# New scheduling priorities for a fused sketch-attention and tanh-shrink kernel

## The chip, the cores and the metric

The kernel runs on one core of a Trainium2 chip. The metric is the time of one execution in microseconds on the device. The time before is the median of three runs.

## The reference

Attention by a polynomial sketch comes first, then a two-layer network on its output. All inputs and the output are float32.

```python
def phi(x):                                   # x: [4, 4, 1088, 32] (batch, head, token, 32)
    a = einsum('rd,bhsd->bhsr', S1, x)        # S1, S2: [8, 32]
    b = einsum('rd,bhsd->bhsr', S2, x)
    return einsum('bhsi,bhsj->bhsij', a, b).reshape(..., 64)
q_p, k_p = phi(q), phi(k)
kv  = einsum('bhsf,bhsd->bhfd', k_p, v)
z   = sum(k_p, axis=2)
num = einsum('bhsf,bhfd->bhsd', q_p, kv)
den = einsum('bhsf,bhf->bhs', q_p, z)[..., None] + 1e-6
x   = (num / den) as [4352, 128]              # tokens x (heads * 32)
h   = x @ w_in                                # w_in: [128, 2048]
out = (h - tanh(h)) @ w_out                   # w_out: [2048, 128]
```

## The kernel before

**What is computed where.** The network is split by linearity: `out = x @ (w_in @ w_out) - tanh(h) @ w_out`. The product of the two weights is formed once, in two bf16 parts (`whi`, `wlo`). So each block of tokens needs matmuls for h (TensorE, line 898), tanh (ScalarE, line 902, with a scale of -1), matmuls of the tanh with `w_out` (line 912), and two linear matmuls with `whi` and `wlo` (line 889).

**Stages.** The 4352 tokens are handled in 11 *layers* of 8 to 14 times 32 tokens (256 to 448 columns). A layer g has 16 blocks jb of the hidden width. The program names its steps by tags, which the text below uses too:

- `h{g}_{jb}`: the matmul of layer g, block jb, into one of three PSUM banks that are used in turn (4, 5, 6). It has to wait until the tanh of three blocks before has left the bank.
- `t{g}_{jb}`: its tanh, into one of 40 slots in SBUF.
- `y{g}_{jb}`: the matmul of the tanh with `w_out`, added up in PSUM bank 7. The linear matmuls are added into the same bank. `o{g}` on VectorE (line 920) turns the sum to the output's layout; four transfers on the queue of SyncE store it.
- The last two layers, 9 and 10, are made in rows of 128 tokens (line 933): `y{g}_{jb}_{y}` and `l{g}_{y}whi`, `l{g}_{y}wlo` for row y, the linear part. Their tokens lie in the last group of the attention, so all of them read what `x8` writes.

The attention feeds this in 9 *groups* of tokens: `qT{g}` transposes q on VectorE (line 695), `p{g}` projects (TensorE, line 717), `qq`, `au`, `dn`, `ds`, `dt`, `rd`, `an`, `qp` and `qpT` (lines 746 to 799, VectorE and GpSimd) make the products and the scaling, `w{g}` (TensorE, line 733) makes the numerators, and `x{g}` (VectorE, line 812) copies them as bf16 into `xT`, which the h and l matmuls read. For `x8`, the last group, the copy has a pattern of its own: it puts the tokens in the order that the rows of the last layers need.

For each of the four batches b there is work on the keys: `kT{b}0`, `kT{b}1` (transposes, VectorE, line 601), `kp{b}` (TensorE, line 608), `kab{b}` (VectorE, line 619), `kps` (line 625), `wk{b}{t}` (products, VectorE and GpSimd, line 634), `gram{b}`, `gm{b}`, `fold{b}`, `u{b}` (lines 645 to 660), `sums{b}` (TensorE, line 673), `kvz{b}`, `turn{b}`, `ndw{b}` (ScalarE and TensorE, lines 681 to 687).

**What sets the order.** Each step is recorded with an engine, a cost in ns, a priority and what it reads and writes. A list scheduler (`listed`) in the kernel's own code then goes through a model of the time: on each engine it takes, of the steps that are ready by the model, the one with the lowest priority value. The order that comes out is fixed in the program; every engine then takes its instructions in that order, with semaphore waits where a step needs one of another engine. Priorities come from the place of a step (for example 16 g + jb for `h`, and 12 more for `y`), and at the end a table adds a shift to some of them:

```python
for tag, by in SHIFT.items():
    P.tags[tag].prio += by
```

The costs that the model uses are formulas; that of a copy on VectorE is

```python
def dve(n):
    return 100 + n / 0.96
```

and `x{g}` is entered at `dve(32 * nb) - 35`, with nb = 20 for `x8`. Some sequences are laid down by hand with `P.line([...])`; these are the same in both kernels.

Of the kernel before, what the change touches and what calls it, by code (L numbers as in the profile page):

```python
# [45 lines left out]
class Program:  # L46
# [210 lines left out]
    def emit(self):  # L257
# [64 lines left out]

SHIFT = {
# [21 lines left out]
}  # L345
TURNED = (0, 1, 3)

# [717 lines left out]
```

## Time and profile before

| | before |
|---|---|
| runs | 102.39, 102.39, 102.28 us; median 102.39 |
| profiled execution | 102.28 us, of which 100.5 are the span of its instructions |
| busy: TensorE, ScalarE, VectorE, GpSimd | 96.5, 78.0, 71.5, 33.2 us |
| matmuls | 1231 |
| tanh instructions (line 902) | 168, 71.9 us |
| granted TensorE clock | 0.996 |

In the profile PE is TensorE's matmuls and PEld its weight loads, DVE is VectorE, ACT ScalarE, POOL GpSimd and SP SyncE. A timeline row has its start and its length in microseconds, the engine, the line in the kernel, the operation with its tiles, and the number of instructions that were merged into the row; in brackets stands the idle time of the engine before it and what ended that. A matmul's length runs to the end of its result, and the next one starts well before that: the pace of PE is read from the starts. A row of the table by stages has start:end, length, and for each engine the busy time with the number of instructions.

### The profile page before, as it was taken

How to read it: one execution, taken by the hardware profiler on the slowest of the kernel's cores; microseconds unless marked ns; L12 is line 12 of the kernel's file. 1: busy time of each engine (PE TensorE's matmuls, PEld its weight loads, DVE VectorE, ACT ScalarE, POOL GpSimd, SP SyncE). 2: the span in 40 equal slices, each digit the busy share in tenths (PEclk: the TensorE clock that was granted, in tenths of full speed). 3: DMA queues.
4: the chain of work that ended last, by engine and by line, in shares of the span. 5: the costliest groups of instructions: out<-in, count | busy, mean ns of one | idle time of the engine just before them, and what ended most of it. 6: DMA issues, size and time to landing. Idle time of an engine off the chain costs nothing.

```text
span 100.5 us, 3032 instructions
## 1 busy us (share of the span) xinstructions
PE 96.5 (96%) x1231; PEld 52.0 (52%) x1231; DVE 71.5 (71%) x181; ACT 78.0 (78%) x182; POOL 33.2 (33%) x60
## 2 busy tenths in 40 slices
PE   6999999999999999999999999999999999999980
PEld 5446467544666444545544444455444444468970
DVE  3689977999869999978999999899577226002140
ACT  0005679998957849793899998898999999999960
POOL 5577388042842400596040029403018000000000
PEclk9999999999999999999999999999999999999998
DMA  2899978920389451310899032002201403100512
GB/s 77 284 281 236 382 237 290 325 66 4 71 285 231 121 91 26 52 33 0 258 273 231 5 49 42 7 0 39 45 14 22 69 0 60 25 0 12 98 42 75
DMA packets 22510, 11.21 MB, mean 112 GB/s; under 512 B 16096, under 2 KB 21216, under 8 KB 22496
## 3 DMA queue, kind: packets, MB, share of 16 engines
q1 hardware_dynamic: 18976, 7.44, 30.5%
q10 hardware_dynamic: 3520, 3.57, 11.5%
q8 instruction: 9, 0.15, 0.6%
q14 instruction: 5, 0.04, 0.1%
HBM read 8.78 MB, written 2.23 MB: 110 GB/s over the span
## 4 chain that ended last, share of the span: by engine, by line
PE 87%; DMA 5%; DVE 4%; ACT 2%; issue 1%; POOL 0%; POOLq 0%; DVEq 0%
PE ps L898 31%; PE ps L912 24%; PE ps L733 5%; PE ps L933 5%; PE ps L673 5%; PE ps L717 4%; PE ps L608 3%; PE ps L889 3%; DMA kraw<-in_k_dram 3%; ACT tt L902 2%; DMA out_dram<-osl 2%; DVE wk L634 1%; PE ps L547 1%; PE ps L849 1%; PE ps L645 1%; PE ps L684 1%
## 5 line engine op out<-in xcount | busy, mean ns | idle before, releaser
L902 ACT ACTIVATE tt<-ps 128x448 bf16<-128x448 f32 (+3 forms) x168 | 71.9, 544 | 6.5 <-PE ps L898 6.0
L898 PE MATMUL ps<-xT,w_in 128*128 128x448 bf16 (+2 forms) x176 | 50.7, 333 | 0.2
L912 PE MATMUL ps<-tt,w_out 128*128 128x448 bf16 (+2 forms) x144 | 39.3, 338 | 0.0
L898 PEld LDWEIGHTS ps<-xT,w_in 128*128 128x128 bf16 x176 | 16.2, 98 | 20.4 <-ACT tt L902 11.5
L634 POOL TENSOR_TENSOR wk<-kab 128x256 f32<-128x256 f32 (+1 forms) x18 | 12.2, 675 | 19.1 <-DVE kab L619 17.5
L792 POOL TENSOR_TENSOR qp<-an,qq 128x512 f32<-128x512 f32 (+5 forms) x12 | 12.4, 1033 | 18.4 <-DVE an L780 17.5
L912 PEld LDWEIGHTS ps<-tt,w_out 128*128 128x128 bf16 x144 | 14.1, 98 | 7.7 <-issue 0.5
L920 DVE STREAM_TRANSPOSE osb<-ps 128x448 f32<-128x448 f32 (+1 forms) x8 | 5.0, 627 | 11.4 <-PE ps L912 11.4
L799 DVE STREAM_TRANSPOSE qpT<-qp 128x448 f32<-128x448 f32 (+5 forms) x18 | 11.4, 658 | 0.3 <-POOL qp L792 0.2
L933 PE MATMUL ps<-w_out,tt 128*128 128x128 bf16 x80 | 8.1, 219 | 0.0
L681 ACT ACT_TABLE_LOAD x1 | 1.3, 1283 | 8.3 <-issue 8.3
L1035 POOL MEMSET mark<- 128x1 f32 x1 | 0.1, 99 | 22.3 <-DMA out_dram<-osl 22.3
L746 DVE STREAM_TRANSPOSE qq<-ps 128x448 f32<-128x448 f32 (+5 forms) x9 | 6.0, 671 | 1.7 <-PE ps L717 1.5
L547 PE MATMUL ps<-const-bfloat16-1.0 128*128 128x256 bf16 (+1 forms) x25 | 6.5, 394 | 0.8 <-PEq L1050 0.8
L812 DVE CAST xT<-ps 128x448 bf16<-128x448 f32 (+4 forms) x8 | 6.2, 773 | 1.5 <-PE ps L733 1.4
L933 PEld LDWEIGHTS ps<-w_out,tt 128*128 128x128 bf16 x80 | 6.4, 98 | 0.6
L601 DVE STREAM_TRANSPOSE kT<-kraw 128x576 f32<-128x576 f32 (+1 forms) x8 | 5.7, 730 | 1.0 <-DMA kraw<-in_k_dram 0.9
L695 DVE STREAM_TRANSPOSE qT<-qraw 128x448 f32<-128x448 f32 (+5 forms) x9 | 5.9, 654 | 0.2 <-DMA qraw<-in_q_dram 0.2
L733 PE MATMUL ps<-qpT,ndw 64*32 64x288 f32 (+5 forms) x144 | 5.7, 373 | 0.0
L717 PE MATMUL ps<-qT,wq 64*32 64x288 f32 (+5 forms) x144 | 5.7, 373 | 0.0
L634 DVE TENSOR_TENSOR wk<-kab,ps 128x512 f32<-128x512 f32 x8 | 5.4, 673 | 0.0
L673 PEld LDWEIGHTS ps<-wk,vx 128*32 128x32 f32 x288 | 4.3, 110 | 1.8 <-issue 1.6
(86 smaller groups left out, 89.0 us busy)
## 6 DMA issues: line engine op xcount, KB each, us to landing
kraw<-in_k_dram SPq DMA_DIRECT2D x3, 544.0 KB, 4.1
qraw<-in_q_dram SPq DMA_DIRECT2D x3, 544.0 KB, 6.0
vx<-in_v_dram SPq DMA_DIRECT2D x10, 144.0 KB, 4.2
out_dram<-osb SPq DMA_DIRECT2D x20, 56.0 KB, 1.9
w_in_f<-in_moe_w_in_dram ACTq DMA_DIRECT2D x2, 512.0 KB, 8.1
w_out_f<-in_moe_w_out_dram ACTq DMA_DIRECT2D x2, 512.0 KB, 8.9
vx<-in_v_dram SPq DMA_DIRECT2D x4, 112.0 KB, 5.6
out_dram<-osb SPq DMA_DIRECT2D x8, 48.0 KB, 1.9
```

The costliest lines, as they stand in the source:

```text
L547: P.op("tensor", 213 if x < 12 else 290, lambda e, n=1 if x < 16 else 2: e.matmul(ps[:, 3, 0:256 * n], ones[:, 0:128], ones[:, None, :].to ...
L634: P.op(eng, 60 + 64 * n if eng == "vector" else pool(64 * n), lambda e: e.tensor_tensor(out=wk[:, t0:t1, :, :].rearrange("p t h (i j) -> p ...
L673: ins = e.matmul(ps[32 * h:32 * h + 32, sbk, 0:64], vx[i][:, h, t, :], wk[:, t, h, :], start=(t == 0), stop=(t == 8), tile_position=(0, 32 ...
L717: ins = e.matmul(o, wq[64 * r:64 * r + 64, b, y, :, :].rearrange("p h x -> p (h x)"), src, start=True, stop=True, tile_position=(64 * r, 3 ...
L733: ins = e.matmul(ps[32 * h:32 * h + 32, 2 + u, 0:32 * nh], ndw[i][64 * u:64 * u + 64, 32 * h:32 * h + 32], src[64 * u:64 * u + 64, h // 2, ...
L792: P.op("vector" if dv else "gpsimd", 95 + 33.2 * m if dv else pool(32 * m), lambda e, lo=lo, dv=dv: e.tensor_tensor(out=qp[u][:, lo:lo + m ...
L799: P.op("vector", dve(32 * m), lambda e, lo=lo: e.transpose(out=qpT[u][:, 32 * lo:32 * (lo + m)], in_=qp[u][:, lo:lo + m, :].rearrange("p n ...
L812: P.op("scalar" if early else "vector", (act if early else dve)(32 * nb) - 35, lambda e: (e.copy if early else e.tensor_copy)(xT[:, x0:x0 ...
L898: P.op("tensor", two * pe(n), lambda e, jb=jb, bk=bk: [e.matmul(bk[:, n * x:n * x + n], w_in[:, 128 * (jb + x):128 * (jb + x) + 128], xT[: ...
L902: P.op("scalar", act(n * two), lambda e, ts=ts, bk=bk: e.activation(out=tt[:, ts:ts + two, 0:n], in_=bk[:, 0:n * two].rearrange("p (x n) - ...
L912: P.op("tensor", pe(n), lambda e, jb=jb, ts=ts: e.matmul(acc[:, 0:n], w_out[:, jb, :], tt[:, ts, 0:n], start=(jb == 0 and g < 2), stop=(jb ...
L933: P.op("tensor", 56, lambda e: e.matmul(ps[:, banks[y], 0:128], lhs, rhs, start=first, stop=last), r=r, w=[bank[banks[y]]], prio=prio, tag ...
```

## The change

Only the table `SHIFT` differs. Of its 148 values 22 change, and 47 entries are added; no step, cost, dependency or hand-written sequence does. The six lines that the table grows by move every later line number by 6. Cut to what the text below speaks of:

```diff
-    "h2_7": 11.5, "h2_10": 11.7, "h2_14": 24.1, "y2_9": 22.0, "y2_12": 26.7, "ds4": -2.0, "kT21": 7.6, "kab2": -3.3,
-    "h3_8": -6.6, "y3_4": 44.0, "y3_9": 63.1, "p5": 35.0, "an5_1": -16.5, "sums20": 321.1, "turn2": 92.7, "h4_9":
+    "h2_7": 42.8, "h2_10": 11.7, "h2_14": 24.1, "y2_9": 48.2, "y2_12": 26.7, "ds4": 8.7, "kT21": 7.6, "kab2": -3.3,
+    "h3_8": -6.6, "y3_4": 44.0, "y3_9": 63.1, "p5": 35.0, "an5_1": -16.5, "sums20": 321.1, "turn2": 54.2, "h4_9":
...
-    "p8": 5.8, "y8_0": 12.1, "y8_7": 22.9, "h9_7": 5.4, "h9_11": -10.6, "h9_13": 26.6, "y9_2_0": 29.9, "y9_7_0":
+    "p8": 59.8, "y8_0": 12.1, "y8_7": 22.9, "h9_7": 5.4, "h9_11": 5.9, "h9_13": 26.6, "y9_2_0": 29.9, "y9_7_0":
...
-    "y10_14_0": 4.3,
+    "y10_14_0": 4.3, "wk10": 46.4, "wt1": -14.5, "ndw1": 10.1, "h2_3": 18.1, "dn4": 11.0, "wk26": -13.6, "gram2":
+    -10.2, "t4_9": -3.9, "y4_3": 43.2, "h5_7": 31.7, "h5_14": 34.2, "y5_7": 30.6, "y6_8": 47.0, "y8_1": 30.7,
+    "y8_8": 30.1, "y9_2_2": -31.1, "y9_7_2": 59.8, "l10_0whi": -8.1, "l10_0wlo": 23.7, "l10_1whi": -5.4, "l10_1wlo":
+    9.3, "y10_7_1": 18.0, "y10_13_1": 54.3, "h2_15": 3.0, "y2_5": 32.5, "w3": -34.1, "kT20": 16.3, "kp2": 267.2,
...
```

What this does to the order: the instructions of each engine stay the same ones. On TensorE the order is the same up to `sums10`, about 30.7 us. On VectorE it changes in two places: `x3`, `qT5`, `kT21` and `o2` go ahead of steps that they followed, and `dn6` goes ahead of `x5`. GpSimd takes `wk26` in the place of `wk24`. ScalarE takes some tanh in another order, and `ndw1` and `ndw2` at other places. The transfers on SyncE's queue keep their order. On TensorE many `h`, `y` and `l` matmuls change places with neighbours, `turn2` and `turn3` go ahead of `p6` and `p8`, and behind `w8` the rows of the last layers are placed anew.

23 rows, old and new, of the table SHIFT are left out of this document.

## The prediction

> **What bounds the kernel now.** I began with the page: its span, the shares of the engines, the chain that ended last and the groups.
>
> ```profile
> span 100.5 us, 3032 instructions
> PE 96.5 (96%) x1231; PEld 52.0 (52%) x1231; DVE 71.5 (71%) x181; ACT 78.0 (78%) x182; POOL 33.2 (33%) x60
> ...
> PE 87%; DMA 5%; DVE 4%; ACT 2%; issue 1%; POOL 0%; POOLq 0%; DVEq 0%
> ...
> L902 ACT ACTIVATE tt<-ps 128x448 bf16<-128x448 f32 (+3 forms) x168 | 71.9, 544 | 6.5 <-PE ps L898 6.0
> ```
>
> The chain runs through PE for 87% of the span. But that is an average, so I looked at the stages next (start and end, length, then busy time and count of each engine).
>
> ```profile
> 30.00:40.00 10.00, 10.00 (x147) 5.05 (x136) 9.69 (x24) 7.60 (x19) 1.91 (x2) 1.00 0.53 123
> 80.00:90.00 10.00, 10.00 (x79) 5.00 (x77) 2.18 (x2) 9.86 (x25) 0.00 (x0) 1.00 0.13 21
> 90.00:95.00 5.00, 5.00 (x64) 4.18 (x62) 0.94 (x2) 5.00 (x17) 0.00 (x0) 1.00 0.30 49
> ```
>
> From 30 to 40 us PE has no gap and ACT is idle for 2.4 us of 10: PE alone sets the pace. From 80 us on both are full. There is no slack left for a PE wait to hide in, on either engine. The timeline of ACT shows how far back that goes (start, length).
>
> ```profile
> 71.49 0.27 ACT L687 COPY ndw<-ps 128x128 f32<-128x128 f32 x1
> 71.68 20.72 ACT L902 ACTIVATE tt<-ps 128x448 bf16<-128x448 f32 x50
> ...
> 83.49 3.54 ACT L902 ACTIVATE tt<-ps 128x448 bf16<-128x448 f32 x8
> ```
>
> From 71.68 us tanh follows tanh. The last row is a shorter window of the same stretch: 3.54 us for 8 tanh is 0.55 for the first and about 0.43 for each that follows.
>
> **What the change can win.** No instruction is added or removed; only the order differs. On PE it is the same until 30.7 us. PE's work is thus the same sum, and the change can only take away waits that PE has now, or add some. The waits of now show as matmuls of 448 columns that start more than 0.19 us after the one before:
>
> ```profile
> 43.32 0.35 PE L898 MATMUL ps<-xT,w_in 128*128 128x448 bf16 x1
> ...
> 44.15 0.36 PE L898 MATMUL ps<-xT,w_in 128*128 128x448 bf16 x1
> ```
>
> Three more such matmuls lie between. The four steps take 0.83 us where 4 x 0.19 = 0.76 would do: 0.07 us lost. Going through the starts of all matmuls up to 83 us I find this cluster and three that are no larger, so at most 0.3 us is to be won there:
>
> ```profile
> 75.62 0.55 PE L898 MATMUL ps<-xT,w_in 128*128 128x384 bf16 x2
> 76.10 0.61 PE L733 MATMUL ps<-qpT,ndw 64*32 64x224 f32 x16
> ```
>
> This one, two matmuls of 384 columns that take 0.48 us ahead of w7, lies where ACT is full. In the changed order the turn of batch 3 (turn3, L684) comes before p8, so its copy on ACT (ndw3, the first row of the ACT timeline above) has its input earlier and holds the following tanh back less. I take 0.06 us as the gain, with bounds 0 and 0.3.
>
> **The moves on VectorE, 36 to 41 us.** Here x3, qT5, kT21 and o2 move up, past dn4, ds4 and dt4.
>
> ```profile
> 36.31 0.76 DVE L812 CAST xT<-ps 128x576 bf16<-128x576 f32 x1
> ...
> 37.77 0.80 DVE L769 COPY ps<-dn 32x32 f32<-32x32 f32 x4
> ...
> 39.24 0.73 DVE L695 STREAM_TRANSPOSE qT<-qraw 128x576 f32<-128x576 f32 x1
> ...
> 39.97 0.57 DVE L920 STREAM_TRANSPOSE osb<-ps 128x384 f32<-128x384 f32 x1
> 40.46 0.74 DVE L619 STREAM_TRANSPOSE kab<-ps 128x576 f32<-128x576 f32 x1
> ...
> 29.34 0.43 SPq L503 DMA_DIRECT2D qraw<-in_q_dram  x1
> ...
> qraw<-in_q_dram SPq DMA_DIRECT2D x1, 544.0 KB, 5.0
> ...
> 39.46 0.71 PE L608 MATMUL ps<-kT,wkm 64*32 64x288 f32 x16
> ```
>
> kab2 is the one that PE waits for next. What precedes it is the same set of instructions, so it starts at about 40.5 us again if nothing waits. Two things could. First, x3 is now issued before dn4, while it still needs w3; w3 is one matmul of layer 2 earlier (0.16 us), and I make the idle time that is left 0 to 0.14 us. Second, qT5 needs batch 2's q: its load was issued at 29.34 and landed 5.0 us later, at 34.3, and qT5 now comes near 36.9. It waits for nothing, and 2.5 us cover it. PE gets one matmul more ahead of kp2, so kab2 has its input at 39.46 + 0.19 + 0.71 = 40.4 us. I take 0 here, bounds 0 and 0.14. The other moves on PE up to 83 us change h and y matmuls of neighbouring blocks about. I added up their starts in the new order, 0.19 us for each of 448 columns, and held them against the ends of the tanh that free their banks: none comes late by more than 0.06 us, and where one does, a wait of now goes. They cost nothing by this sum. The moves on GpSimd swap wk24 with wk26, of equal size, and cost nothing, as sums20 waits for all of them.
>
> **The move that costs: the tail of layer 8.** The old order on PE after w8 (L733) and the new one, by the program's names:
>
> ```
> before: h8_9 . h8_10 . h8_11 y8_0 h8_12 y8_1 h8_13 y8_2 h8_14 y8_3 l9_1whi h8_15 l9_1wlo y8_4 h9_0
> after:  h8_9 . h8_10 . h8_11 y8_0 h8_12 l9_1whi l9_1wlo h8_13 l10_0whi l10_1whi y8_1 h8_14 y8_2 h8_15 y8_3 y8_4 h9_0
> ```
>
> A dot is a linear matmul of layer 8. The four l matmuls moved up read xT of the last two layers, which is written by x8, the cast after w8 on VectorE:
>
> ```profile
> 82.39 0.77 PE L733 MATMUL ps<-qpT,ndw 64*32 64x320 f32 x16
> 83.09 0.36 PE L898 MATMUL ps<-xT,w_in 128*128 128x448 bf16 x1
> ...
> 84.23 0.35 PE L898 MATMUL ps<-xT,w_in 128*128 128x448 bf16 x1
> 84.42 0.35 PE L912 MATMUL ps<-tt,w_out 128*128 128x448 bf16 x1
> 84.61 0.35 PE L898 MATMUL ps<-xT,w_in 128*128 128x448 bf16 x1
> ...
> 85.37 0.22 PE L933 MATMUL ps<-whi,xT 128*128 128x128 bf16 x1
> 85.42 0.35 PE L898 MATMUL ps<-xT,w_in 128*128 128x448 bf16 x1
> ...
> 85.86 0.33 PE L898 MATMUL ps<-xT,w_in 128*128 128x384 bf16 x1
> ```
> ```profile
> 83.27 1.59 DVE L812 CAST xT<-ps 128x640 bf16<-128x640 f32 x1 [0.31 <-PE ps L733]
> ```
>
> x8 ends at 83.27 + 1.59 = 84.86 us. Now l9_1whi starts at 85.37, half a microsecond after it. In the new order its place comes right after h8_12 (84.23), at 84.42: 0.44 us before xT is there. PE takes its instructions in order, so h8_13, which needs nothing from x8, stands behind that wait. How soon PE goes on after VectorE is seen at another such wait, o2: it ended at 39.97 + 0.57 = 40.54, and the weight load that waited for it started at 40.59:
>
> ```profile
> 40.59 0.10 PEld L889 LDWEIGHTS ps<-xT,whi 128*128 128x128 bf16 x1 [0.18 <-DVE osb L920]
> ```
>
> So l9_1whi starts at about 84.92, and PE waits 0.50 us. The planner in the code counts x8 at 100 + 640/0.96 - 35 = 732 ns and would see no wait there; the trace has 1,592 ns.
>
> [...]
>
> **What the wait does to the end.** h8_13 comes after the two l matmuls of layer 9 (0.055 us each, as from 85.37 to 85.42): 84.92 + 0.11 = 85.03, against 84.61 now. Then h8_14 comes at 85.03 + 0.19 + 0.11 + 0.19 = 85.52, h8_15 at 85.90, h9_0 at 86.47, and on in this way. How long a tanh takes from its matmul is read where ACT was idle before it:
>
> ```profile
> 47.24 0.73 PE L898 MATMUL ps<-xT,w_in 128*128 128x448 bf16 x3
> ...
> 47.63 0.98 ACT L902 ACTIVATE tt<-ps 128x448 bf16<-128x448 f32 x2 [0.78 <-PE ps L898]
> ```
>
> The first of the three matmuls started at 47.24 and the first tanh at 47.63: 0.39 us. ACT reaches the tanh of h8_13 at 83.49 + 4 x 0.43 = 85.2 now. In the new order its input allows 85.03 + 0.39 = 85.42: ACT idles for 0.2 us. The tanh of h8_14 can start at 85.91, 0.05 later than ACT could; h9_0 and then h9_4, which stands behind two matmuls of y8, add about 0.05 each. After h9_4 the three banks of h set the pace again. ACT is then 0.35 us late. The other 0.15 us of the wait is absorbed, since PE had been ahead of the banks there. ACT is full from there to the end, so the 0.35 us stay.
>
> The end itself changes too:
>
> ```profile
> 96.44 0.28 PE L898 MATMUL ps<-xT,w_in 128*128 128x256 bf16 x1
> 96.56 1.11 PE L933 MATMUL ps<-w_out,tt 128*128 128x128 bf16 x17
> ...
> 97.54 0.49 DVE L942 COPY osl<-ps 128x128 f32<-128x128 f32 x2 [0.99 <-PE ps L933]
> ```
>
> After the last h (96.44, freed by ACT) PE now has 17 row matmuls; in the new order 19 are left. Two more at 0.055 us put the last copy 0.11 us later.
>
> **The sum.** -0.06 (waits that go) + 0 (VectorE) + 0.35 (x8) + 0.11 (rows) = +0.40 us. The profiled execution took 102.28 us, its span 100.5 and 1.78 around it; it would take 102.68. It is the lowest of the runs, 0.11 below their median, so I forecast 102.39 + 0.40 = 102.8 us.
>
> **The rivals.** (1) The wait for x8 is not there, or ACT doesn't feel it. For it: the same instruction at 576 columns needs far less, and x8 may have been slow in this one execution. Against it: the long cast is the only one with the strided pattern of the last group in the code, so I expect the 1.59 us each time. Then -0.06 + 0.11 = +0.05: 102.4 us.
>
> ```profile
> L812 DVE CAST xT<-ps 128x576 bf16<-128x576 f32 x2 | 1.5, 758 | 0.1
> ```
>
> (2) Faster: the earlier stages win all the 0.3 us and x8 is no obstacle either; then -0.3 + 0.11 = -0.19, and 102.2 us. It decides if x8 ends before 84.37 us, since only then l9_1whi finds it done. (3) Slower by more: x3 holds up VectorE by 0.14 us, fold2 and w4 are late by as much, and on top comes the whole wait of 0.50, if PE was not ahead after all: 0.14 + 0.50 + 0.11 = 0.75, or 103.1 us. For it speaks that qpT40 is ready only 0.18 us before w4 takes it:
>
> ```profile
> 43.85 1.30 DVE L799 STREAM_TRANSPOSE qpT<-qp 128x512 f32<-128x512 f32 x2
> ...
> 45.33 0.64 PE L733 MATMUL ps<-qpT,ndw 64*32 64x256 f32 x16
> ```
>
> Against it: the PE waits that go just ahead of w4 (0.07 us, above) would pay half of the delay.
>
> **How the numbers follow.** Forecast 60%, rival 1 20%, rival 2 10%, rival 3 10%. The range runs from rival 1 with a small credit, 102.35, to rival 3, 103.15; that leaves rival 2 and a little of each end out. A difference of 0.2% (0.2 us) is about what a measurement here can tell from none. Slower by more: most of the forecast (0.54), rival 3 (0.10) and the upper end of rival 1 (0.04): 0.68. Within: the rest of the forecast and most of rival 1, 0.20. Faster: rival 2 and the lower end of rival 1, 0.12.
>
> **What would show it.** In the new profile: right after h8_12 a weight load of whi that waited about 0.45 us for the cast of xT on VectorE; an idle stretch of 0.2 us on ACT near 85.2 us, in the midst of what is now one unbroken row; 19 row matmuls behind the last h. Up to 83 us the two timelines should agree within 0.15 us. The prediction is wrong if l9_1whi starts without a wait, or if the last h comes at 96.4 us in spite of it.

## The result and the profile after

| | before | changed |
|---|---|---|
| runs | 15, median 102.39 us | 15, median 102.80 us |
| ratio of the two | | 1.004, 95% interval 1.0023 to 1.0057 |
| profiled execution | 102.28 us, span 100.5 | 103.18 us, span 101.4 |

The kernel is slower by 0.4%, and a ratio of 1 lies outside the interval. The forecast was 102.8 us. The two profiled executions differ by more than the medians, 0.9 us, so they can't be set side by side as they stand. The page of the changed kernel shows what is new in its chain:

```profile
PE 89%; DVE 5%; ACT 2%; DMA 2%; issue 1%; POOL 0%; POOLq 0%
PE ps L904 30%; PE ps L918 24%; PE ps L739 5%; PE ps L939 5%; PE ps L679 5%; PE ps L553 5%; PE ps L723 4%; PE ps L614 3%; PE ps L895 3%; ACT tt L908 2%; DMA out_dram<-osl 2%; DVE xT L818 2%; DVE wk L640 1%; PE ps L855 1%; PE ps L651 1%; PE ps L841 1%
```

`DVE xT L818 2%` is the cast x8 (every line number is 6 higher now; in the kernels of the experiments the numbers differ again, and the tiles tell which line it is). Its 1.58 us lie on the path that sets the end; in the chain before, no cast of VectorE was listed. PE's timeline shows the place, the weight loads and VectorE's cast with it:

```profile
84.50 0.35 PE L918 MATMUL ps<-tt,w_out 128*128 128x448 bf16 x1
84.69 0.35 PE L904 MATMUL ps<-xT,w_in 128*128 128x448 bf16 x1
85.36 0.23 PE L939 MATMUL ps<-whi,xT 128*128 128x128 bf16 x1 [0.32 <-DVE xT L818]
85.42 0.22 PE L939 MATMUL ps<-wlo,xT 128*128 128x128 bf16 x1
85.48 0.35 PE L904 MATMUL ps<-xT,w_in 128*128 128x448 bf16 x1
```
```profile
85.35 0.10 PEld L939 LDWEIGHTS ps<-whi,xT 128*128 128x128 bf16 x1 [0.72 <-DVE xT L818]
```
```profile
83.72 1.58 DVE L818 CAST xT<-ps 128x640 bf16<-128x640 f32 x1 [0.31 <-PE ps L739]
```

h8_12 starts at 84.69 and l9_1whi at 85.36: 0.67 us, of which 0.19 are h8_12 itself. PE waited 0.48 us (the bracket has 0.32, as the result of h8_12 still runs out in that time; that of the weight load has 0.72, as the load before it, for h8_12, had ended earlier). The cast ended at 83.72 + 1.58 = 85.30, and the weight load came 0.05 us after it.

**Where to count from.** The order is the same up to sums10, yet sums10 starts at 30.07 us in this profile and at 29.53 in the one before. That 0.5 us is not the change's. I count from the start of sums10 to the end of the last row matmul in each profile:

```profile
29.53 1.21 PE L673 MATMUL ps<-wk,vx 128*32 128x64 f32 x72
```
```profile
30.07 1.21 PE L679 MATMUL ps<-wk,vx 128*32 128x64 f32 x72
...
97.23 0.28 PE L904 MATMUL ps<-xT,w_in 128*128 128x256 bf16 x1
97.35 1.23 PE L939 MATMUL ps<-w_out,tt 128*128 128x128 bf16 x19
```

Before: 96.56 + 1.11 - 29.53 = 68.14 us. Changed: 97.35 + 1.23 - 30.07 = 68.51 us. The change costs 0.37 us in this count, near the 0.41 of the medians. With the 0.54 us up to sums10 it makes up the 0.9 us between the two profiled executions. The last row also shows the 19 row matmuls behind the last h, in the place of 17.

### The profile page after: what moved, and what is told of

Its sections match the earlier page's. It is cut to its first block, busy times and chain, and to the rows that moved or that the text cites. A ratio compares the mean times of both kernels' runs of the same rounds, so it can differ in the third digit from the quotient of the medians.

```text
span 101.4 us, 3031 instructions
## 1 busy us (share of the span) xinstructions
PE 97.0 (96%) x1231; PEld 52.2 (51%) x1231; DVE 71.5 (71%) x181; ACT 78.3 (77%) x182; POOL 33.2 (33%) x60
## 4 chain that ended last, share of the span: by engine, by line
PE 89%; DVE 5%; ACT 2%; DMA 2%; issue 1%; POOL 0%; POOLq 0%
PE ps L904 30%; PE ps L918 24%; PE ps L739 5%; PE ps L939 5%; PE ps L679 5%; PE ps L553 5%; PE ps L723 4%; PE ps L614 3%; PE ps L895 3%; ACT tt L908 2%; DMA out_dram<-osl 2%; DVE xT L818 2%; DVE wk L640 1%; PE ps L855 1%; PE ps L651 1%; PE ps L841 1%
## 5 line engine op out<-in xcount | busy, mean ns | idle before, releaser
L818 DVE CAST xT<-ps 128x448 bf16<-128x448 f32 (+4 forms) x8 | 6.2, 771 | 1.7 <-PE ps L739 1.7
L939 PE MATMUL ps<-w_out,tt 128*128 128x128 bf16 x80 | 7.3, 219 | 0.0
```

Source lines behind the costliest of these rows:

```text
L818: P.op("scalar" if early else "vector", (act if early else dve)(32 * nb) - 35, lambda e: (e.copy if early else e.tensor_copy)(xT[:, x0:x0 ...
L939: P.op("tensor", 56, lambda e: e.matmul(ps[:, banks[y], 0:128], lhs, rhs, start=first, stop=last), r=r, w=[bank[banks[y]]], prio=prio, tag ...
```

## The experiments

Theory A is the one of the prediction: the l matmuls moved up wait for x8. B puts the loss into the moves between 31 and 83 us or into the early loads. C says that the new tail costs as a whole, whatever those four matmuls do. Three columns tell them apart: the ratio of times, the count from sums10 in one profile, and x8's length there.

| kernel | ratio to before (95%) | from sums10 to the end, against before (us) | x8 (us) |
|---|---|---|---|
| changed | 1.004 (1.0023 to 1.0057) | 68.51, +0.37 | 1.58 |
| changed, old tail | 0.9997 (0.9972 to 1.0022) | 68.07, -0.07 | 1.59 |
| before, new tail | 1.0026 (1.0005 to 1.0046) | 68.59, +0.45 | 1.58 |
| changed, four l back | 0.9991 (0.9965 to 1.0017) | 68.17, +0.03 | 1.58 |
| changed, x8 dense | 0.9999 (0.9974 to 1.0024) | 68.16, +0.02 | 0.82 |
| before, four l early | 1.0051 (1.0024 to 1.0077) | 68.70, +0.56 | 1.58 |
| before, x8 dense | 0.9995 (0.9972 to 1.0017) | 68.13, -0.01 | 0.82 |
| changed, planner knows x8 | 0.9999 (0.9978 to 1.0020) | 68.10, -0.04 | 1.59 |
| changed, x8 twice | 1.0170 (1.0145 to 1.0194) | 69.86, +1.72 | 1.59 and 1.61 |
| before, four l early, h8_13 ahead | a single run, no interval | 68.70, +0.56 | 1.58 |

**The two halves of the change.** In the kernels that have another tail, TensorE's order behind h8_12 is exchanged after the planner has run (`TAIL` lists the names in the order wanted):

```diff
         order = self.schedule()
+        pe = order["tensor"]
+        at = pe.index(self.tags["h8_12"]) + 1
+        moved = [self.tags[x] for x in TAIL]
+        assert set(moved) == set(pe[at:])
+        order["tensor"] = pe[:at] + moved
         self.sync(order)
```

The changed kernel with the old tail:

> The changed kernel with the old order of TensorE behind h8_12 (all other orders as changed). Theory A (the l matmuls stand waiting for x8, and two more rows are left at the end): the whole loss lies behind h8_12, 0.35 + 0.11 us, and the stages before it are 0.06 to 0.09 us quicker than in the kernel before. So 0.05 to 0.1 us below the kernel before, ratio about 0.999, against 1.004 for the change. Theory B (the loss comes from the moves between 31 and 83 us, or from the early loads): it stays at about +0.4 us, ratio 1.004.

The kernel before with the new tail:

> The kernel before with the new order of TensorE behind h8_12, and nothing else of the change. Theory A: the wait of about 0.5 us of l9_1whi for x8 appears here too, and 0.35 + 0.11 = 0.46 us are lost: ratio 1.0045. Theory B: no difference from the kernel before, ratio 1.000.

The loss went with the tail, both ways: -0.07 us without it, +0.45 us with nothing but it. The two profiles:

```profile
29.65 1.21 PE L697 MATMUL ps<-wk,vx 128*32 128x64 f32 x72
...
96.61 1.11 PE L957 MATMUL ps<-w_out,tt 128*128 128x128 bf16 x17
```
```profile
29.54 1.21 PE L691 MATMUL ps<-wk,vx 128*32 128x64 f32 x72
...
96.79 0.28 PE L916 MATMUL ps<-xT,w_in 128*128 128x256 bf16 x1
96.91 1.22 PE L951 MATMUL ps<-w_out,tt 128*128 128x128 bf16 x19
```

B falls. The times agree, less sharply: the ratio of the kernel before with the new tail, 1.0026, is 0.27 us, with 0.05 to 0.47 as its interval. The 0.07 us of gain in the earlier stages shows only in this count; the interval of the times can't tell it from none.

**Only the four l matmuls put back.** l9_1whi and l9_1wlo stand around h8_15 again, l10_0whi and l10_1whi ahead of l10_1wlo; the rest of the new tail stays.

> The changed kernel with only four matmuls put back: l9_1whi and l9_1wlo around h8_15 as before, l10_0whi and l10_1whi ahead of l10_1wlo. Theory A: the wait for x8 goes and with it 0.35 us; the 0.11 us for two more rows at the end stay, and so does the gain of 0.06 to 0.09 in the earlier stages: +0.02 to +0.05 us, ratio about 1.000. Theory C (the rest of the new tail, the y8 matmuls put off and the rows, costs as much by itself): +0.3 to +0.4 us, ratio 1.003 to 1.004.

```profile
84.09 0.65 PE L922 MATMUL ps<-xT,w_in 128*128 128x448 bf16 x2
84.58 0.35 PE L936 MATMUL ps<-tt,w_out 128*128 128x448 bf16 x1
84.81 0.36 PE L922 MATMUL ps<-xT,w_in 128*128 128x448 bf16 x1
85.01 0.35 PE L936 MATMUL ps<-tt,w_out 128*128 128x448 bf16 x1
85.20 0.22 PE L957 MATMUL ps<-whi,xT 128*128 128x128 bf16 x1
```
```profile
83.79 0.97 ACT L926 ACTIVATE tt<-ps 128x448 bf16<-128x448 f32 x2
```

The loss is gone to 0.03 us, so C falls as well. The rows also show that PE idles a little in this tail: h8_12 and h8_13 need 0.49 us from 84.09 to 84.58 where 0.38 would do (two steps of 0.19, as from 84.50 to 84.69 in the changed kernel), and y8_1 0.23 instead of 0.19. With less y8 work ahead of them the h matmuls run up against their banks: the tanh of h8_11 ended at 83.79 + 0.97 = 84.76 us, and h8_14, which uses its bank next, started at 84.81. PE idles 0.15 us there. When the wait for x8 is there, it takes the place of this idling: the last h of the changed kernel comes 0.33 us later than the one here (67.16 against 66.83 us after sums10), which is 0.48 less 0.15.

**x8 made short.** The cast goes through its elements in the order of xT, so it writes densely and reads PSUM with a stride (lines shortened):

```diff
-            xT[...].rearrange("p (y j u c) -> p u y c j", j=32, u=2, c=2),
+            xT[...].rearrange("p (y j u c) -> p y j u c", j=32, u=2, c=2),
-            ps[:, 2:4, 0:32 * nh].rearrange("p u (y c j) -> p u y c j", c=2, j=32)
+            ps[:, 2:4, 0:32 * nh].rearrange("p u (y c j) -> p y j u c", c=2, j=32)
```

> The changed kernel with the same order, where the cast x8 goes through its elements so that it writes xT densely and reads PSUM with a stride (the same values at the same places). Theory A: if the scattered write is why x8 takes 1.59 us, it now takes 0.75 to 0.85 us and ends before l9_1whi's turn; the wait goes, and 0.35 us with it: ratio about 1.000. If the strided read costs as much as the scattered write, x8 stays near 1.6 us and the time at +0.4 us. Theory B: x8 may get shorter and the time stays at +0.4 us.

> The kernel before with the dense cast x8 (about 0.82 us in place of 1.59), order unchanged. Theory A: nothing waits for x8 here, since l9_1whi's turn came 0.5 us after its end; so the time is the same, ratio 1.000, and the dense cast's gain in the changed kernel came from the wait alone. Rival: the shorter cast is worth 0.3 us by itself, ratio 0.997.

```profile
83.95 0.82 DVE L818 CAST xT<-ps 128x640 bf16<-128x640 f32 x1 [0.31 <-PE ps L739]
```
```profile
84.92 0.35 PE L904 MATMUL ps<-xT,w_in 128*128 128x448 bf16 x1
85.11 0.22 PE L939 MATMUL ps<-whi,xT 128*128 128x128 bf16 x1
85.16 0.22 PE L939 MATMUL ps<-wlo,xT 128*128 128x128 bf16 x1
```

The cast halves to 0.82 us, l9_1whi follows h8_12 without a gap (84.92 to 85.11), and the loss is gone though the order is that of the change. In the kernel before the same shorter cast gives nothing, as nothing waited for it there. So it is the wait that costs, not the cast.

**x8 made later.** A copy into a spare tile goes ahead of the cast, and VectorE's order stays (shortened):

```diff
+                for to in (spare[:, :], xT[:, x0:x0 + 32 * nb]):
+                    ins = e.tensor_copy(to.rearrange("p (y j u c) -> p u y c j", j=32, u=2, c=2), ...)
```

> The changed kernel with the cast x8 made twice, first into a spare tile of the same pattern, then into xT; the order on every engine is as in the change. Theory A: xT comes about 1.55 us later, l9_1whi waits 2.0 us instead of 0.5, and as neither PE nor ACT has slack behind it, nearly all of that reaches the end: 1.9 us over the kernel before, ratio 1.019. Theory B (the wait is covered and the loss comes from elsewhere): much less than 1.5 us more than the change.

```profile
83.28 1.59 DVE L822 CAST spare<-ps 128x640 bf16<-128x640 f32 x1 [0.31 <-PE ps L740]
84.67 1.61 DVE L822 CAST xT<-ps 128x640 bf16<-128x640 f32 x1
```
```profile
84.25 0.35 PE L910 MATMUL ps<-xT,w_in 128*128 128x448 bf16 x1
86.34 0.23 PE L945 MATMUL ps<-whi,xT 128*128 128x128 bf16 x1 [1.74 <-DVE xT L822]
```

xT came 1.35 us later than in the change, counted from sums10, not 1.55: two such casts behind each other overlap, the second starts 1.39 us after the first. The end came 69.86 - 68.51 = 1.35 us later. All of what came on top arrived: beyond the 0.15 us of the change nothing in this tail hid a wait of PE.

**The planner told the truth.** One number in the changed kernel (line shortened):

```diff
-        P.op(..., (act if early else dve)(32 * nb) - 35, ...
+        P.op(..., 1592 if g == NG - 1 else (act if early else dve)(32 * nb) - 35, ...
```

> The changed kernel with one number of the planner corrected: x8 is entered at the 1,592 ns that the trace shows, not 732. The planner itself then puts l9_1whi behind y8_3 again, as in the kernel before, and the l10 pair behind h9_1; the rows at the end stay 19. Theory A: the wait goes, ratio 1.000 (+0.02 to +0.05 us). Theory C: +0.3 us or more, ratio 1.003.

The planner moves l9_1whi behind y8_3 by itself, where the kernel before has it, and the loss is gone (-0.04 us by the count). With the same number the priorities of before give just the order of before, by the planner's output; no time was taken of that.

**The four l matmuls early, in the old tail.**

> The kernel before with one thing done: l9_1whi and l9_1wlo right behind h8_12, l10_0whi and l10_1whi right behind h8_13, as in the change; everything else as before, the end with 17 rows too. Theory A: l9_1whi waits 0.5 us for x8, and 0.3 to 0.35 us of it reach the end: ratio 1.003, last row matmul 0.3 to 0.35 us later counted from sums10. Theory C (the tail costs as a whole, not by these four): ratio 1.000.

They cost more here than I expected: 0.56 us. I thought that y8_1, which stood ahead of h8_13 in this kernel, was the reason, and moved it behind:

> As the run with the four l matmuls early in the kernel before, but with h8_13 ahead of y8_1, as the change has it. That run lost 0.56 us counted from sums10 to the last row, not 0.35. If the reason is that h8_13 stood behind y8_1 as well and came 0.61 us late instead of 0.42, h8_13 is now 0.42 us late, ScalarE's delay shrinks by 0.19, and the last row comes 0.37 to 0.45 us later than in the kernel before. If the whole PE wait of 0.48 us is lost in any order of this tail, it stays at 0.5 us or more.

```profile
29.76 1.21 PE L691 MATMUL ps<-wk,vx 128*32 128x64 f32 x72
...
97.23 0.28 PE L916 MATMUL ps<-xT,w_in 128*128 128x256 bf16 x1
97.35 1.11 PE L951 MATMUL ps<-w_out,tt 128*128 128x128 bf16 x17
```

It made no difference, 68.70 us again: my reason was wrong. Both kernels have y8_1 and y8_2 ahead of h8_14, and in both its tanh ends 0.43 us later than before, counted from sums10 (57.11 against 56.68). The new tail puts y8_2 behind h8_14; there it is 56.92, 0.24 later. The lead is still there at the last h: 96.79 - 29.54 = 67.25 us after sums10 with the new tail, 97.23 - 29.76 = 67.47 here. Putting off y8 work so seems to spare ScalarE some 0.2 us of the wait, and two rows at the end pay 0.11 of it back. That no further order was tried leaves this part argued, not shown.

No kernel here beats the one before by more than its interval. The best count, -0.07 us, is the change with the old tail.

## Why the prediction was right

- **The wait for x8.** Forecast 0.50 us at l9_1whi; it was 0.48. The shorter cast and the longer one show that this wait makes the loss, and rival 1 (the cast slow in one execution only) is out: x8 took 1.58 to 1.61 us in every profile that kept its pattern.
- **What of it reaches the end.** Forecast 0.35 us through ScalarE and 0.11 by the two rows. From sums10 the last h comes at 97.23 - 30.07 = 67.16 us, against 96.44 - 29.53 = 66.91: 0.25 later, though w8 came 0.09 earlier, so 0.34 are lost behind w8. From that h to the end it takes 1.35 us in place of 1.23: 0.12 for the two rows. The kernel before with the new tail lost 0.45 in sum by the count, against 0.46. What ScalarE was to lose near 85.2 us shows too, though no bracket has it: the tanh of h8_12 and h8_13 take 1.00 us together before and 1.18 with the change, 0.18 more where 0.2 was expected.

```profile
84.78 1.00 ACT L902 ACTIVATE tt<-ps 128x448 bf16<-128x448 f32 x2
```
```profile
85.23 1.18 ACT L908 ACTIVATE tt<-ps 128x448 bf16<-128x448 f32 x2
```

- **The gain of the earlier stages.** Forecast 0.06 us; the old tail on the change gives -0.07. Rival 2, which wanted 0.3, had no such sum to win. But the reason was not the one I gave. I had ndw3 hold back the tanh behind it and so the two matmuls ahead of w7. Those two still take 0.48 us (76.07 to 76.55), and the tanh started 0.39 us after its matmul before (71.68 - 71.29) and 0.40 with the change (72.13 - 71.73): the time that a tanh takes from its matmul, so ndw3 held up nothing. What became shorter is PE's own time where turn3 now goes ahead of p8: from the two h in front of the pair to the h behind it, 71.73 - 70.45 = 1.28 us in place of 71.29 - 69.95 = 1.34. Where turn2 goes ahead of p6 it is the same 0.06 (1.17 in place of 1.23), a place that the prediction did not name. Why this order of the two is shorter no run shows. So the size came near by luck.

```profile
69.95 0.54 PE L898 MATMUL ps<-xT,w_in 128*128 128x448 bf16 x2
70.43 0.77 PE L717 MATMUL ps<-qT,wq 64*32 64x320 f32 x16
71.13 0.33 PE L684 MATMUL ps<-ident,kvz 128*128 128x128 f32 x1
71.29 0.35 PE L898 MATMUL ps<-xT,w_in 128*128 128x448 bf16 x1
```
```profile
70.45 0.54 PE L904 MATMUL ps<-xT,w_in 128*128 128x448 bf16 x2
...
71.73 0.36 PE L904 MATMUL ps<-xT,w_in 128*128 128x448 bf16 x1
...
76.07 0.55 PE L904 MATMUL ps<-xT,w_in 128*128 128x384 bf16 x2
76.55 0.61 PE L739 MATMUL ps<-qpT,ndw 64*32 64x224 f32 x16
...
82.84 0.77 PE L739 MATMUL ps<-qpT,ndw 64*32 64x320 f32 x16
```
```profile
71.70 0.32 ACT L693 COPY ndw<-ps 128x128 f32<-128x128 f32 x1
72.13 25.88 ACT L908 ACTIVATE tt<-ps 128x448 bf16<-128x448 f32 x67
```

- **The moves on VectorE.** Forecast 0, with 0 to 0.14 as bounds. VectorE idled 0.17 us for x3, a little over the bound, and kab2 came 0.09 us later from sums10 (41.09 - 30.07 = 11.02, against 40.46 - 29.53 = 10.93). It reached nothing: w4 came at the same distance from sums10 to 0.02 us (45.88 - 30.07 = 15.81, against 45.33 - 29.53 = 15.80). Rival 3 did not happen.

```profile
36.69 0.76 DVE L818 CAST xT<-ps 128x576 bf16<-128x576 f32 x1 [0.17 <-PE ps L739]
...
41.09 0.78 DVE L625 STREAM_TRANSPOSE kab<-ps 128x576 f32<-128x576 f32 x1
```

- **What was off.** I said that the two timelines would agree within 0.15 us up to 83 us. They differ by half a microsecond from before sums10 on, with the same order on TensorE. Counted from sums10 they agree at w8: it comes 82.84 - 30.07 = 52.77 us after sums10, and 82.39 - 29.53 = 52.86 before the change. That the median fell on 102.8 us to the tenth is partly luck too: the interval of the ratio lets the loss be anything from 0.24 to 0.58 us.

## What to carry to other kernels

Where two engines are full to the end, find each point at which the new order lets an engine wait for a third one, and compare the start of its turn with the end of what it waits for, by the trace's durations and not by the planner's. One instruction whose cost the planner had at less than half (732 ns, against 1,592 in the trace) was enough here: the planner moved work onto just that spot, because by its costs the spot was free. Before comparing two profiles, find a step up to which the programs are the same, and count from it.

## What the runs showed of the hardware

The same 128x640 cast, 640 elements in each partition, took VectorE 1.58 to 1.61 us with 2-byte writes scattered over xT and contiguous reads from PSUM, and 0.82 us with dense writes and strided reads; by these rows the stride on the reading side costs little if anything, since 576 elements without any stride took 0.76 us, from which I estimate 0.84 for 640 by the number of elements.

The stretch up to sums10, in the same order on every engine until there, ended between 29.46 us (four l put back) and 30.30 us (x8 dense) in single profiles. This spread of 0.84 us is twice what the change moves; what makes it no run shows. From sums10 to w8, kernels with the same order agree within 0.1 us: x8, which follows w8, starts 53.73 to 53.74 us after sums10 in four profiles with the order of before, and 53.58 to 53.67 in six with that of the change.
